# Bucket attention with a rational feed-forward layer on one core: row maxima transposed before they are clamped, bucket rows scaled on ScalarE, GpSimd's sums of exponentials made head by head

## Chip, cores and metric

The kernel runs on one core of one Trainium2 chip. The metric is the device time of one execution in microseconds (us). Three runs of the kernel before gave 1029.2, 1029.55 and 1035.9 us, median 1029.55 us.

## What is computed

Two stages follow each other. The first is attention within hash buckets, for 4 batches of 8 heads, 768 positions, 64 dimensions:

```python
q_bits = (np.einsum('bhsd,dk->bhsk', q, proj) > 0)        # 6 bits; k_bits the same
q_bucket = np.sum(q_bits * 2 ** np.arange(6), axis=-1)
mask = q_bucket[:, :, :, None] == k_bucket[:, :, None, :]
scores = np.where(mask, scale * (q @ k.T), -1e9)
scores = scores - np.max(scores, axis=-1, keepdims=True)
attn = np.exp(scores); attn = attn / (np.sum(attn, axis=-1, keepdims=True) + 1e-09)
x = attn @ v                                               # then heads side by side: 3072 x 512
```

The second is a feed-forward layer whose activation is a quotient of two polynomials:

```python
h = x @ w_in                                               # 512 -> 2048
g = (a0 + a1*h + a2*h*h + a3*h**3) / (1 + abs(b0)*abs(h) + abs(b1)*h*h + 1e-6)
out = g @ w_out                                            # 2048 -> 512
```

## The kernel before

**Pairs and steps.** The 32 heads are worked on as 16 pairs p = 0 to 15. A pair's attention takes 12 steps: step s is half `hf` of the queries (384 columns) and key tile `kt` (128 keys). In a step `scores` (L248) makes, for each of the two heads h, a product `pss` in PSUM, and ScalarE turns it into exponentials E (L256). GpSimd adds the exponentials of three key tiles into a tile `acc` (L263, one instruction for both heads, 128 x 768). `values` (L265) multiplies E by V into `psv`. In the middle pairs these come two steps at a time, so a group of eight `psv` records marks two steps on TensorE. `sums` (L284) adds up `acc` over the partitions into `psu`, once for each pair.

**The mask and the maximum ride in the product.** Operand tiles Q1 and K1 hold 64 rows of q or k, 12 rows of bucket bits scaled by plus or minus 2^60 (L209), and one row more, row 76, with the shift that is subtracted from the scores (L242). `bits` (L188) makes the bucket rows of two pairs at once, in every second pair: 16 small products into `psb`, then on VectorE a comparison out of PSUM into the tile `mb` (L202) and a multiplication of `mb` in place by a column of constants (L203). `maskrows` (L205) copies the rows into Q1 and K1 by DMA.

**The shift.** `maxstep` (L212) makes unmasked-scale products `psm` a pair and more ahead, and a VectorE reduction writes the row maxima into a tile M[p], 128 x 12 (L220; m in the profile). Its PSUM pool has two buffers, so TensorE's second next `psm` waits for a reduction. Then three functions follow:

- `shift_clamp` (L223): VectorE limits the maxima from below and negates them, SBUF to SBUF, into a tile nm of 128 x 12;
- `shift_turn` (L231): TensorE transposes nm into a PSUM tile `pst` of 12 x 128 (L234), ScalarE copies it to the tile mt (L236);
- `shift_rows` (L238): a DMA lays mt out as row 76 of Q1.

For pair 0 the three run twice, on one half of the queries each (`hf` 0 and 1, tiles of 128 x 6), since its maxima are made in another order (L433).

**Weights beside it.** `weights` (L319), spread over the steps, splits the weights into a high and a low part: two ScalarE passes, then on VectorE three integer passes (tiles wr and ws, L339 to L345), a ScalarE cast, and a subtraction (L351, to wi_lo or wr). There are two such sets for each pair. Also on VectorE are the low parts `lo` of q and k (L174), with two SBUF inputs.

**What sets the order.** Every compute instruction is kept in program order on its engine. The order comes from a table `plan`: `at(p, s, f)` files the call f under 12p + s, and the calls are made in order of that number, within one number in order of filing. For pair p the table has maxima 0 to 11 from step 7 of pair p-2 on (L373), the clamp at step 7 of pair p-1, the turn at step 8 and the DMA at step 10 (L400 to L402). For pair 0 the second half's clamp stands at 0.5 and its turn at 2 (L438 to L440).

**The second stage** (`Ffn`, L507) starts when attention is over; its 128 steps keep TensorE at work without the functions above.

In the profile nearly every instruction has line L61, that of the helper `issued` (L60 to L61); it is read by the names of the tiles, where numbers of buffers are left out. The functions that the diff touches:

Of the kernel before, what the change touches and what calls it, by code (L numbers as in the profile page):

```python
# [7 lines left out]
F32 = mybir.dt.float32  # L8
# [3 lines left out]
AF = mybir.ActivationFunctionType  # L12
ALU = mybir.AluOpType
# [4 lines left out]
P = 128  # L18
S = 768
HQ = 384  # L20
NT = S // P
# [13 lines left out]
CLAMP = 2.0 ** 40  # L35
# [30 lines left out]
def move(nc, out, in_, queue=None):  # L66

    (queue or nc.sync).dma_start(out.bitcast(F32), in_.bitcast(F32))
# [69 lines left out]
def attention(ctx, tc, nc, raw, ps_b, tail, tokens, early, operands_to_terms, ffn, load, QF, KF, v, w_in, w_out, wo_d, ident, cst, ones, prj,  # L138
# [9 lines left out]
    sm = ctx.enter_context(tc.tile_pool(name="sm", bufs=1))  # L148
# [5 lines left out]
    Q1, Q2, K1, K2, LO, V, M, MB, ACC, EXP, AV, MS = ({} for _ in range(12))  # L154

    def load_v(p, queue=nc.sync):
        V[p] = operand("v", p, [P, NT, P], F32)
        queue.dma_start(V[p], v[p])
# [8 lines left out]
    def high_move(p):  # L167
        for T, g in ((Q1[p], 0), (K1[p], 1)):
            move(nc, T[0:64, 1 - g, :], T[64:128, g, :])

    def low(p, t, engine=nc.vector):
        F, T = ((QF, Q1), (KF, K1))[t]
        LO[p, t] = raw.tile([P, S], F32R, tag=f"lo{t}", name=f"lo{t}_{p}", bufs=1)
        engine.tensor_tensor(out=LO[p, t], in0=F[p], in1=T[p][:, t, :].bitcast(F32), op=ALU.subtract)  # L174
# [13 lines left out]
    def bits(p, which=(0, 1)):  # L188

        if which[0] == 0:  # L190
            mb = sm.tile([P, 2, HQ], F32R, tag="mb", name=f"mb{p}")
            MB[p], MB[p + 1] = (mb, 0), (mb, 64)
        mb = MB[p + which[0]][0]
        sl = slice(64 * which[0], 64 * which[-1] + 64)
        ps = ps_a.tile([P, 2, 512], F32, tag="psa", name=f"psb{p}_{which[0]}")
        for hf in range(2):
            for w in which:
                for t, F in enumerate((QF[p + w], KF[p + w])):
                    o = 64 * w + 32 * t
                    nc.tensor.matmul(ps[o : o + 32, hf, 0:HQ], prj[:, t, :], F[:, hf * HQ : hf * HQ + HQ], start=True, stop=True)  # L200
        rows = mb[sl]
        nc.vector.tensor_scalar(out=rows, in0=ps[sl, :, 0:HQ], scalar1=0.0, scalar2=cst[sl, 0:1], op0=ALU.is_gt, op1=ALU.subtract)  # L202
        nc.vector.tensor_scalar(out=rows, in0=rows.bitcast(F32), scalar1=cst[sl, 1:2], scalar2=None, op0=ALU.mult)  # L203

    def maskrows(p, queues=(None, None)):  # L205
        mb, o = MB.pop(p)
# [13 lines left out]
        nc.vector.tensor_reduce(out=M[p][:, j : j + 1], in_=ps[:, :, 0:HQ], axis=AX.XY, op=ALU.max)  # L220


    def shift_clamp(p, hf=None):  # L223
        m = M[p].rearrange("p (h f i) -> p h f i", h=2, f=2)
        m = m if hf is None else m[:, :, hf : hf + 1, :]
        n = NT if hf is not None else 2 * NT
        MS[p] = sm.tile([P, n], F32, tag="nm", name=f"nm{p}_{hf}")
        nc.vector.tensor_scalar(out=MS[p].rearrange("p (h f i) -> p h f i", h=2, i=NT // 2), in0=m, scalar1=-CLAMP, scalar2=-1.0,
                                op0=ALU.max, op1=ALU.mult)

    def shift_turn(p, hf=None):  # L231
        n = NT if hf is not None else 2 * NT
        ps = ps_b.tile([P, 512], F32, tag="s", bufs=3, name=f"pst{p}_{hf}")
        nc.tensor.transpose(ps[0:n, 0:P], MS.pop(p), ident)  # L234
        MS[p] = sm.tile([n, P], F32R, tag="mt", name=f"mt{p}_{hf}")
        nc.scalar.copy(MS[p], ps[0:n, 0:P])  # L236

    def shift_rows(p, hf=None):  # L238
        cs = slice(0, S) if hf is None else slice(hf * HQ, hf * HQ + HQ)
# [8 lines left out]
    def scores(p, s):  # L248
        hf, kt = divmod(s, NT)
        e = EXP[p, s] = E[(12 * p + s) % len(E)]  # L250
        ks, qs = slice(kt * P, kt * P + P), slice(hf * HQ, hf * HQ + HQ)
        for h in range(2):
            ps = ps_b.tile([P, 512], F32, tag="s", bufs=3, name=f"pss{p}_{s}_{h}")
            nc.tensor.matmul(ps[:, 0:HQ], K1[p][0:77, h, ks], Q1[p][0:77, h, qs], start=True, stop=False)
            nc.tensor.matmul(ps[:, 0:HQ], K2[p][:, h, ks], Q2[p][:, h, qs], start=False, stop=True)
            nc.scalar.activation(e[:, h, 0:HQ], ps[:, 0:HQ], AF.Exp, scale=1.0 / 8.0)  # L256
        n = NT // PARTS
        if kt % n == 1:
            ACC[p, hf, kt // n] = sm.tile([P, 2, HQ], F32, tag="acc", name=f"acc{p}_{hf}_{kt // n}", bufs=ACCS)
        if kt % n > 0:  # L260
            acc = ACC[p, hf, kt // n]
            x = EXP[p, s - 1][:, :, 0:HQ] if kt % n == 1 else acc
            nc.gpsimd.tensor_tensor(out=acc, in0=x, in1=e[:, :, 0:HQ], op=ALU.add)  # L263

    def values(p, s):  # L265
        hf, kt = divmod(s, NT)
# [94 lines left out]
    def at(p, s, f, *args):  # L361
        plan.setdefault(12 * p + s, []).append((f, args))

    def spread(p, steps, gen):
        for s in steps:
            at(p, s, lambda g: next(g, None), gen)

    for p in range(NPAIR):
        for s in range(12):
            at(p, s, scores, p, s)  # L370

            if p > 1:
                at(p - 2, 7 + s if p > 2 else 9 + 0.85 * s, maxstep, p, s)  # L373

            if not 0 < p < NPAIR - 1:
                at(p, s + 2.3, values, p, s)
            elif s % 2:
                at(p, s + 1.3, values, p, s - 1)
                at(p, s + 1.3, values, p, s)
            if s % NT == NT - 1:  # L380
                at(p, s + (1.3 if 0 < p < NPAIR - 1 else 2.3), values_out, p, s // NT)
        for hf in range(2):
            at(p, 6 * hf + 9, values_store, p, hf)
        if p < NPAIR - 1:
            at(p, 14.5, sums, p)
            at(p, 16, sums_store, p)
        if p > 1:
            for t in range(2):
                at(p - 2, t, high, p, t)
                at(p - 2, 2 + t, low, p, t)  # L390
            if p % 2 == 0:
                at(p - 2, 3 if p == 2 else 2, bits, p)
            at(p - 2, 2, high_move, p)
            at(p - 2, 6 if p == 2 else 4, maskrows, p)
        if p > 0:
            at(p - 1, 0, second_low, p)
            at(p - 1, 3, second_high, p)
            at(p - 1, 4, load_v, p)
            d = 1.5 if p == 1 else 0
            at(p - 1, 7 + d, shift_clamp, p)  # L400
            at(p - 1, 8 + d, shift_turn, p)
            at(p - 1, 10 if d == 0 else 9.6, shift_rows, p)  # L402
        if p > 3:
            at(p - 4, 6, load, p)
        if p % NHP == NHP - 1 and p + 1 < NPAIR:
            spread(p, (20, 22, 23), recips(p // NHP))
# [12 lines left out]
    for t in range(2):  # L419
        high(0, t)  # L420
        low(0, t)
    bits(0, (0,))
    high_move(0)
    maskrows(0, (nc.sync, nc.scalar))
    load(2, nc.scalar)
    load_v(0, nc.scalar)
    bits(0, (1,))
    for t in range(2):
        high(1, t)
    second_low(0)  # L430
# [5 lines left out]
        at(-2, when[s], maxstep, 0, order[s])  # L436
        at(0, 0.6 + 0.7 * s, maxstep, 1, s)
    for hf in range(2):  # L438
        for s, f in ((5, shift_clamp), (6.5, shift_turn), (6.6, shift_rows)):
            at(-2, 19.5 * hf + s, f, 0, hf)  # L440
    for t in range(2):
        low(1, t, nc.gpsimd)
# [211 lines left out]
```

## Time and profile before

| | |
|---|---|
| median of three runs | 1029.55 us (1029.2 to 1035.9) |
| profiled execution | 1029.27 us, its span 1027.5 us |
| TensorE busy | 977.0 us (95%) |
| VectorE busy | 907.9 us (88%) |
| ScalarE busy | 678.9 us (66%) |
| GpSimd busy | 384.8 us (37%) |
| mean granted TensorE clock | 0.971 |

The names of the engines in the profile are PE (TensorE matmul), PEld (its weight loads), DVE (VectorE), ACT (ScalarE), POOL (GpSimd) and SP (the engine that issues most DMAs). The span has three parts: about 55 us of start, in which pair 0's operands are made and its first scores come; the attention proper to about 490 us; and the second stage to the end. A row of a timeline reads: start, duration, engine, operation, output <- inputs, shapes, count, and in brackets how long the engine had been idle and what released it. A row of the groups reads: shapes and count, then busy us and mean ns of one, then idle time before them. A row of windows gives for each engine its busy us and (x) its instructions, then the granted clock (PEclk, 1.00 is full), the DMA share and GB/s.

### The profile page before, as it was taken

What the parts mean: (1) busy time and instruction counts of PE and PEld (TensorE: products, weight loads), DVE (VectorE), ACT (ScalarE), POOL (GpSimd) and SP (SyncE); (2) the same over time, 40 slices, a digit from 0 to 9 for tenths busy, and PEclk for the clock granted to TensorE, in tenths of its full rate; (3) what the DMA queues carried; (4) which work ended last, traced back from release to release, by engine and by line L of the source; (5) the groups of instructions that cost most, each with busy time, mean ns of one, the idle gap of its engine ahead of it and who ended that gap; (6) DMA issues with size and microseconds to landing.
All of it is one profiled execution on the core that took longest, in us unless ns stands there. A gap on an engine that the chain in (4) does not pass through costs nothing.

```text
span 1027.5 us, 14486 instructions
## 1 busy us (share of the span) xinstructions
PE 977.0 (95%) x5009; PEld 749.4 (73%) x5009; DVE 907.9 (88%) x1207; ACT 678.9 (66%) x1419; POOL 384.8 (37%) x268
## 2 busy tenths in 40 slices
PE   6899988989898988999999999999999999999998
PEld 2565555555555555564999999999999999999996
DVE  5688788878978787767999999999999999999996
ACT  1466555656656655567877777777777777777775
POOL 1255554545545454556222222222222222222222
PEclk7799999999999999899999999999999999999999
DMA  7765564656656664673740201101111010020000
GB/s 202 195 165 175 165 177 124 177 163 186 187 165 211 206 205 134 177 217 118 283 137 15 69 11 62 32 1 62 32 57 36 1 62 31 1 72 22 32 1 31
DMA packets 50489, 112.95 MB, mean 110 GB/s; under 512 B 9296, under 2 KB 21968, under 8 KB 50416
## 3 DMA queue, kind: packets, MB, share of 16 engines
q1 hardware_dynamic: 49580, 110.59, 35.8%
q10 hardware_dynamic: 836, 1.44, 0.5%
q8 instruction: 39, 0.64, 0.3%
q14 instruction: 34, 0.28, 0.1%
HBM read 56.82 MB, written 21.17 MB: 76 GB/s over the span
## 4 chain that ended last, share of the span: by engine, by line
PE 78%; DVE 13%; DMA 3%; issue 2%; ACT 2%; SPq 1%; DVEq 0%; ACTq 0%
PE psh L61 26%; PE pso L61 26%; PE psv L61 10%; PE pss L61 9%; PE psm L61 4%; DVE m L61 3%; DVE wr L61 2%; DVE ws L61 2%; DVE nm_None L61 2%; PE psu L61 2%; DVE wi_lo L61 2%; ACT E L61 1%; DMA k<-k 1%; PE psb L61 1%; SPq L61 1%
## 5 line engine op out<-in xcount | busy, mean ns | idle before, releaser
L61 POOL TENSOR_TENSOR gl<-c,gh 128x384 fp32r<-128x384 f32 x128 | 140.6, 1099 | 396.0 <-ACT gh L61 369.4
L61 DVE TENSOR_REDUCE m<-psm 128x1 f32<-128x768 f32 x192 | 180.1, 949 | 76.8 <-PE psm L61 76.2
L61 PE MATMUL pso<-wo,gh 128*128 128x512 f32 x768 | 241.1, 395 | 0.0
L61 ACT ACTIVATE E<-pss 128x384 f32<-128x384 f32 x384 | 168.4, 490 | 97.9 <-PE pss L61 92.4
L61 POOL TENSOR_TENSOR acc<-E,E 128x768 f32<-128x768 f32 x64 | 126.2, 1972 | 190.3 <-ACT E L61 190.3
L61 PE MATMUL pss<-q,k 77*128 77x384 f32 (+1 forms) x768 | 183.1, 361 | 3.0 <-DMA q<-mt 2.6
L61 PEld LDWEIGHTS pss<-q,k 77*128 77x128 f32 (+1 forms) x768 | 136.7, 196 | 64.6 <-issue 54.4
L61 PE MATMUL psh<-xl,wi_hi 128*128 128x384 f32 x512 | 172.1, 336 | 0.0
L61 PE MATMUL psh<-xh,wi_hi 128*128 128x384 f32 x512 | 171.7, 335 | 0.0
L61 PE MATMUL psh<-xh,wi_lo 128*128 128x384 f32 x512 | 171.5, 335 | 0.0
L61 PEld LDWEIGHTS pso<-wo,gh 128*128 128x128 f32 x768 | 142.9, 188 | 23.7
L61 PE MATMUL psv<-E,v 128*64 128x385 f32 x768 | 157.3, 529 | 0.0
L61 PE MATMUL pso<-wo,gl 128*128 128x512 f32 x384 | 152.2, 396 | 0.3 <-POOL gl L61 0.3
L61 DVE SCALAR_TENSOR_TENSOR c<-c,ab,r 128x384 f32<-128x384 f32 x128 | 147.1, 1149 | 0.0
L61 ACT ACTIVATE h<-psh 128x384 f32<-128x384 f32 x128 | 63.1, 493 | 122.4 <-PE psh L61 122.4
L61 POOL TENSOR_TENSOR acc<-acc,E 128x768 f32<-128x768 f32 x64 | 113.9, 1780 | 30.1 <-ACT E L61 27.5
L61 PE MATMUL psm<-k,q 76*128 76x384 f32 x384 | 111.1, 374 | 13.9 <-DVE m L61 9.8
L61 PEld LDWEIGHTS psh<-xh,wi_hi 128*128 128x128 f32 x512 | 96.1, 188 | 6.3 <-issue 1.2
L61 PEld LDWEIGHTS psh<-xl,wi_hi 128*128 128x128 f32 x512 | 96.0, 188 | 5.1
L61 PEld LDWEIGHTS psh<-xh,wi_lo 128*128 128x128 f32 x512 | 96.1, 188 | 0.0
L61 PEld LDWEIGHTS psm<-k,q 76*128 76x128 f32 x384 | 71.7, 204 | 31.8 <-DVE m L61 22.2
L61 PEld LDWEIGHTS psv<-E,v 128*64 128x64 f32 x768 | 47.6, 141 | 64.1 <-issue 56.7
(63 smaller groups left out, 1322.6 us busy)
## 6 DMA issues: line engine op xcount, KB each, us to landing
q<-q SPq DMA_DIRECT2D x48, 192.0 KB
k<-k SPq DMA_DIRECT2D x48, 192.0 KB
wr<-w_in SPq DMA_DIRECT2D x16, 512.0 KB
wr<-w_out SPq DMA_DIRECT2D x16, 512.0 KB
wo_d<-wr SPq DMA_DIRECT2D x16, 512.0 KB
wo<-wo_d SPq DMA_DIRECT2D x16, 512.0 KB
q<-lo SPq DMA_DIRECT2D x32, 192.0 KB
k<-lo SPq DMA_DIRECT2D x32, 192.0 KB
```

The costliest lines, as they stand in the source:

```text
L61: return self.tc.keep_in_program_order(issue(*args, **kwargs))
```

## The change

1. **Turn, then clamp.** `shift_clamp` is gone. `shift_turn` transposes the maxima themselves, and a VectorE instruction clamps and negates them on the way out of PSUM, in place of ScalarE's copy. For pair 0's halves a VectorE copy first picks 6 of the 12 columns.
2. **Scaling on ScalarE.** The multiplication of the bucket rows becomes a ScalarE activation in a function `penalties`, one step after `bits`.
3. **Sums by heads.** GpSimd adds each head's 384 columns by an instruction of its own.

```diff
-        rows = mb[sl]
-        nc.vector.tensor_scalar(out=rows, in0=ps[sl, :, 0:HQ], scalar1=0.0, scalar2=cst[sl, 0:1], op0=ALU.is_gt, op1=ALU.subtract)
-        nc.vector.tensor_scalar(out=rows, in0=rows.bitcast(F32), scalar1=cst[sl, 1:2], scalar2=None, op0=ALU.mult)
+        nc.vector.tensor_scalar(out=mb[sl], in0=ps[sl, :, 0:HQ], scalar1=0.0, scalar2=cst[sl, 0:1], op0=ALU.is_gt, op1=ALU.subtract)
+
+    def penalties(p, which=(0, 1)):
+        sl = slice(64 * which[0], 64 * which[-1] + 64)
+        rows = MB[p + which[0]][0][sl]
+        nc.scalar.activation(rows, rows.bitcast(F32), AF.Identity, scale=cst[sl, 1:2])
...
-    def shift_clamp(p, hf=None):
-        m = M[p].rearrange("p (h f i) -> p h f i", h=2, f=2)
-        m = m if hf is None else m[:, :, hf : hf + 1, :]
-        n = NT if hf is not None else 2 * NT
-        MS[p] = sm.tile([P, n], F32, tag="nm", name=f"nm{p}_{hf}")
-        nc.vector.tensor_scalar(out=MS[p].rearrange("p (h f i) -> p h f i", h=2, i=NT // 2), in0=m, scalar1=-CLAMP, scalar2=-1.0,
-                                op0=ALU.max, op1=ALU.mult)
-
     def shift_turn(p, hf=None):
-        n = NT if hf is not None else 2 * NT
+        n, m = 2 * NT, M[p]
+        if hf is not None:
+            n, m = NT, sm.tile([P, NT], F32, tag="nm", name=f"nm{p}_{hf}")
+            nc.vector.tensor_copy(m.rearrange("p (h i) -> p h i", h=2), M[p].rearrange("p (h f i) -> p h f i", h=2, f=2)[:, :, hf, :])
         ps = ps_b.tile([P, 512], F32, tag="s", bufs=3, name=f"pst{p}_{hf}")
-        nc.tensor.transpose(ps[0:n, 0:P], MS.pop(p), ident)
+        nc.tensor.transpose(ps[0:n, 0:P], m, ident)
         MS[p] = sm.tile([n, P], F32R, tag="mt", name=f"mt{p}_{hf}")
-        nc.scalar.copy(MS[p], ps[0:n, 0:P])
+        nc.vector.tensor_scalar(out=MS[p], in0=ps[0:n, 0:P], scalar1=-CLAMP, scalar2=-1.0, op0=ALU.max, op1=ALU.mult)
...
-            x = EXP[p, s - 1][:, :, 0:HQ] if kt % n == 1 else acc
-            nc.gpsimd.tensor_tensor(out=acc, in0=x, in1=e[:, :, 0:HQ], op=ALU.add)
+            x = EXP[p, s - 1] if kt % n == 1 else acc
+            for h in range(2):
+                nc.gpsimd.tensor_tensor(out=acc[:, h, :], in0=x[:, h, 0:HQ], in1=e[:, h, 0:HQ], op=ALU.add)
...
                 at(p - 2, 3 if p == 2 else 2, bits, p)
+                at(p - 2, 4 if p == 2 else 3, penalties, p)
...
-            at(p - 1, 7 + d, shift_clamp, p)
             at(p - 1, 8 + d, shift_turn, p)
...
     bits(0, (0,))
+    penalties(0, (0,))
...
     bits(0, (1,))
+    penalties(0, (1,))
...
-        for s, f in ((5, shift_clamp), (6.5, shift_turn), (6.6, shift_rows)):
+        for s, f in ((6.5, shift_turn), (6.6, shift_rows)):
             at(-2, 19.5 * hf + s, f, 0, hf)
```

How this moves instructions is shown at three places.

**VectorE, steps 6 to 8 of pair 2**, where the maxima of pair 3 (m3) are complete and those of pair 4 begin. ISA is one of the passes over the weights. Before:

```order
L61 SCALAR_TENSOR_TENSOR ws4_870<-ws4_870,wr4_869 128x512
L61 TENSOR_REDUCE m3_743<-psm3_11_989 128x1
L61 ISA ws4_870<-wr4_869,ws4_870 128x1024
L61 TENSOR_SCALAR nm3_None_1016<-m3_743 128x12
L61 TENSOR_REDUCE m4_1018<-psm4_0_1019 128x1
L61 TENSOR_REDUCE m4_1018<-psm4_1_1040 128x1
```

And now:

```order
L61 SCALAR_TENSOR_TENSOR ws4_883<-ws4_883,wr4_882 128x512
L61 TENSOR_REDUCE m3_752<-psm3_11_1005 128x1
L61 ISA ws4_883<-wr4_882,ws4_883 128x1024
L61 TENSOR_REDUCE m4_1033<-psm4_0_1034 128x1
L61 TENSOR_SCALAR mt3_None_1054<-pst3_None_1052 12x128
L61 TENSOR_REDUCE m4_1033<-psm4_1_1056 128x1
```

The clamp has moved behind the first reduction of the next pair, and its input is now the transposed tile in PSUM, so that it follows TensorE where it used to go ahead of it.

**TensorE at the same place.** Before, and below it now:

```order
L61 MATMUL psm4_0_1019<-k1_4_867,q1_4_842 128x384 x2
L61 MATMUL pss2_8_0_1027<-q1_2_290,k1_2_313 128x384
L61 MATMUL pss2_8_0_1027<-q2_2_563,k2_2_564 128x384
L61 MATMUL pss2_8_1_1031<-q1_2_290,k1_2_313 128x384
L61 MATMUL pss2_8_1_1031<-q2_2_563,k2_2_564 128x384
L61 MATMUL pst3_None_1036<-cst_76,nm3_None_1016 12x128
```

```order
L61 MATMUL psm4_0_1034<-k1_4_880,q1_4_854 128x384 x2
L61 MATMUL pss2_8_0_1042<-q1_2_290,k1_2_312 128x384
L61 MATMUL pss2_8_0_1042<-q2_2_569,k2_2_570 128x384
L61 MATMUL pss2_8_1_1046<-q1_2_290,k1_2_312 128x384
L61 MATMUL pss2_8_1_1046<-q2_2_569,k2_2_570 128x384
L61 MATMUL pst3_None_1052<-cst_76,m3_752 12x128
```

The order is the same; the transposition's input is m3 itself, complete since the reduction of psm3_11, and no longer the clamped nm3.

**VectorE at the start, second half of pair 0** (m0, nm0_1), among the maxima of pair 1 (m1) and the low part of pair 2's q (lo0_2). Before:

```order
L61 TENSOR_REDUCE m0_215<-psm0_11_292 128x1
L61 TENSOR_SCALAR nm0_1_296<-m0_215 128x6
L61 TENSOR_REDUCE m1_298<-psm1_0_299 128x1
L61 TENSOR_REDUCE m1_298<-psm1_1_318 128x1
L61 TENSOR_TENSOR lo0_2_331<-qf2_182,q1_2_290 128x768
L61 TENSOR_REDUCE m1_298<-psm1_2_335 128x1
L61 TENSOR_REDUCE m1_298<-psm1_3_348 128x1
```

And now:

```order
L61 TENSOR_REDUCE m0_215<-psm0_11_292 128x1
L61 TENSOR_REDUCE m1_296<-psm1_0_297 128x1
L61 TENSOR_REDUCE m1_296<-psm1_1_317 128x1
L61 TENSOR_TENSOR lo0_2_331<-qf2_182,q1_2_290 128x768
L61 TENSOR_REDUCE m1_296<-psm1_2_335 128x1
L61 COPY nm0_1_339<-m0_215 128x6
L61 TENSOR_SCALAR mt0_1_343<-pst0_1_341 6x128
L61 TENSOR_REDUCE m1_296<-psm1_3_350 128x1
```

The instruction that feeds pair 0's second transposition has moved from ahead of lo0_2 to behind it and behind one more reduction; TensorE's order there is as it was (psm1_2, the transposition pst0_1, psv0_0, psm1_3).

## Prediction

> **What bounds the kernel now.** I read the windows first, to see which stage is filled by which engine.
>
> ```profile
> 55.00:445.00 390.00, 356.03 (x1952) 219.37 (x1952) 322.74 (x339) 230.57 (x512) 201.63 (x109) 0.96 0.60 175
> 445.00:490.00 45.00, 44.61 (x248) 25.17 (x237) 32.83 (x29) 31.38 (x71) 28.01 (x15) 1.00 0.52 164
> 490.00:1027.00 537.00, 533.50 (x2667) 480.43 (x2665) 517.10 (x798) 399.08 (x803) 140.63 (x128) 1.00 0.15 49
> ```
>
> The last 537 us are TensorE without a gap (533.5 busy, full clock) and hold nothing that is changed. From 55 to 445 us TensorE is idle for 34 us and its clock averages 0.96. That stage is where time can be won. The waits say what TensorE idles for:
>
> ```profile
> PE pst_None L61 <- DVE nm_None L61: 23.4, 13, 1.9
> PE psm L61 <- DVE m L61: 9.8, 18, 0.8
> DVE m L61 <- PE psm L61: 76.2, 47, 4.0
> ```
>
> 23.4 us, 13 times, up to 1.9 us each, are transpositions that wait for the clamp. The third row is the other direction: VectorE waits 76 us for products, so on the whole it follows TensorE. The timeline at one of the 13 places shows why the clamp is late:
>
> ```profile
> 307.81 0.87 ACT L61 ACTIVATE E<-pss 128x384 f32<-128x384 f32 x2
> 308.17 0.87 PE L61 MATMUL pss<-q,k 77*128 77x384 f32 x4
> 308.75 1.97 POOL L61 TENSOR_TENSOR acc<-E,E 128x768 f32<-128x768 f32 x1 [2.92 <-ACT E L61]
> 308.98 1.77 DVE L61 TENSOR_SCALAR nm_None<-m 128x12 f32<-128x12 f32 x1
> 310.67 1.85 DVE L61 TENSOR_REDUCE m<-psm 128x1 f32<-128x768 f32 x2
> 310.90 0.27 PE L61 MATMUL pst_None<-cst,nm_None 128*12 128x128 f32 x1 [1.87 <-DVE nm_None L61]
> 311.20 0.26 ACT L61 CAST mt_None<-pst_None 12x128 fp32r<-12x128 f32 x1 [0.73 <-PE pst_None L61]
> ```
>
> TensorE ends pss at 309.04 and could turn the maxima there. The clamp, over 12 columns, lasts 1.77 us and ends at 310.75, with GpSimd's addition (308.75 + 1.97 = 310.72). It is not work, it is held:
>
> ```profile
> L61 DVE TENSOR_SCALAR nm_None<-m x15: 160/1775/1779, 53.8 to 454.7; 128x12 f32<-128x12 f32 x15
> L61 DVE TENSOR_SCALAR mb<-psb,cst x9: 1004/1006/1023, 8.9 to 383.4; 128x768 fp32r<-128x768 f32 x7, 64x768 fp32r<-64x768 f32 x2
> L61 DVE TENSOR_SCALAR mb<-mb,cst x9: 612/994/996, 9.9 to 384.4; 128x768 fp32r<-128x768 f32 x7, 64x768 fp32r<-64x768 f32 x2
> ```
>
> (minimum, median, maximum in ns.) The same clamp takes 160 ns when free and 1775 when held. Of the two passes over mb, the one out of PSUM always takes 1.0 us, the one within SBUF 612 or 994. So a VectorE instruction of this kind that reads SBUF waits for a running GpSimd addition, and one that reads PSUM does not.
>
> The wait has a second price. These are windows of 3.41 us each:
>
> ```profile
> 162.97:166.38 3.41, 1.56 (x10) 0.98 (x10) 3.41 (x5) 2.06 (x6) 2.84 (x2) 1.00 0.47 173
> 166.38:169.80 3.42, 3.42 (x11) 1.60 (x8) 0.81 (x1) 0.01 (x1) 0.79 (x1) 0.50 0.03 9
> 193.69:197.10 3.41, 1.91 (x11) 0.82 (x11) 3.11 (x3) 1.33 (x4) 3.01 (x2) 1.00 0.58 205
> 197.10:200.51 3.41, 3.41 (x20) 2.56 (x20) 1.97 (x3) 2.49 (x6) 0.66 (x1) 1.00 0.01 2
> ```
>
> Where the clamp's wait falls so that TensorE is busy for 1.56 of 3.41 us, the next window has half the clock; where 1.91 us are left it has not. Over 55 to 445 us the mean of 0.96 means 2 x 0.04 x 390 = 31 us at half clock, nine such windows. What one costs is seen in the starts of the psv groups, two steps apart:
>
> ```profile
> 275.99 1.51 PE L61 MATMUL psv<-E,v 128*64 128x385 f32 x8
> 281.88 2.33 PE L61 MATMUL psv<-E,v 128*64 128x385 f32 x8
> 287.21 1.51 PE L61 MATMUL psv<-E,v 128*64 128x385 f32 x8
> 292.04 1.51 PE L61 MATMUL psv<-E,v 128*64 128x385 f32 x8
> 295.79 1.51 PE L61 MATMUL psv<-E,v 128*64 128x385 f32 x8
> ```
>
> The last distance, 3.75 us, is undisturbed. The first, 5.89, holds the transposition and its wait; the second, 5.33, the half clock; the third, 4.83, a wait for reductions that came late after it.
>
> **The change part by part.**
>
> *Turn, then clamp.* The transposition now waits for the maxima alone, which were complete one VectorE pass before 308.98. Its PSUM buffer is that of an exponential of the row at 307.81, free at 308.68, before pss ends. So the 23.4 us go: **-23.4**. The new clamp is nearest in size to ScalarE's copy of the same tile, 0.26 us, and reads PSUM, so it is not held. In VectorE's queue it stands behind a reduction of 0.95 us that starts at about 309.0, and the transposition (309.05 + 0.27) is done before that ends. No wait is added there, and the DMA that lays out the shift is ready at about 310.3 instead of 311.46.
>
> *The clock.* Without the 1.9 us holes no window falls to 1.6 us of work; the next largest waits are 0.8. Nine windows at half speed lose 31 x 0.5 = 15.6 us: **-15.6**. Below that it is nothing, if the holes are not what halves the clock; above, 2.6 a window (5.33 + 4.83 - 2 x 3.75), counted partly in the next term.
>
> The Trainium skill (TensorE: Matmul & The Clock Gate, "What's actually happening") has the clock halved after at least one idle window of about 3.4 us. By that rule waits of 1.9 us cost no clock and this term is nothing. The rows above disagree, since a window with 1.56 us of work was enough; the rule is kept as a rival below.
>
> *GpSimd's halves.* The group rows bound a piece of 384 columns:
>
> ```profile
> L61 POOL TENSOR_TENSOR gl<-c,gh 128x384 fp32r<-128x384 f32 x128 | 140.6, 1099 | 396.0 <-ACT gh L61 369.4 <-PE psh L61 19.1 <-issue 7.5
> L61 POOL TENSOR_TENSOR acc<-E,E 128x768 f32<-128x768 f32 x64 | 126.2, 1972 | 190.3 <-ACT E L61 190.3
> L61 POOL TENSOR_TENSOR acc<-acc,E 128x768 f32<-128x768 f32 x64 | 113.9, 1780 | 30.1 <-ACT E L61 27.5 <-ACT absb L61 1.1
> ```
>
> Between 0.89 (half of 1780) and 1.10; I take 1.0. 256 x 1.0 is 256 us for 240 now (126.2 + 113.9), over a stage in which GpSimd is half idle, and the first half starts one exponential (0.43 us) earlier: no cost; without that cover 16 us. The gain is on VectorE:
>
> ```profile
> 301.33 2.20 POOL L61 TENSOR_TENSOR acc<-E,E 128x768 f32<-128x768 f32 x1 [1.90 <-ACT E L61]
> 301.77 2.32 DVE L61 TENSOR_TENSOR wr<-ws,wr 128x512 fp32r<-128x512 f32 x1
> 305.01 0.61 PE L61 MATMUL psm<-k,q 76*128 76x384 f32 x2 [0.55 <-DVE m L61]
> L61 DVE TENSOR_TENSOR wr<-ws,wr x16: 680/689/2329, 287.1 to 487.3; 128x512 fp32r<-128x512 f32 x16
> ```
>
> A pass of 0.69 us (median) lasts 2.32 behind an addition, the reduction behind it is late, and psm waits 0.55 us for its buffer. Held by half an addition, the pass ends about 0.7 us earlier, more than that wait. The waits for m are 9.8 us in all, some of them the aftermath of half clocks. Bounds 0 (the halves run on without letting VectorE in between) and 9.8; I take two thirds: **-6.5**.
>
> The Trainium skill (SBUF — State Buffer, "Who interferes with whom") says that whoever issues first holds the shared port pair for the whole instruction. By it VectorE gets in between two halves, and the term would be the full 9.8.
>
> *Scaling on ScalarE.* VectorE loses nine passes of 0.6 to 1.0 us. ScalarE gains nine, nearest to its cast of a 128x768 tile:
>
> ```profile
> L61 ACT CAST q<-qf 128x768 fp32r<-128x768 f32 x16 | 13.3, 832 | 10.3 <-DMA k<-mb 8.1 <-DMA qf<-qT 2.2
> 328.03 1.86 ACT L61 ACTIVATE E<-pss 128x384 f32<-128x384 f32 x4
> 329.60 0.79 SPq L61 DMA_DIRECT2D q<-mb  x1
> ```
>
> The new pass stands behind the second of those exponentials (328.96), so mb is ready at 329.8 and SP, which issues its copies at 329.60 and has loads for pairs far ahead queued behind them, is 0.2 us late. The next exponentials wait 0.83 us; ScalarE is busy 231 of 390 us, which covers it. Taken at nothing; uncovered, 9 x 0.83 = 7.5 us.
>
> *The start.* Here the change costs. Pair 0's second half is clamped early today, and now its copy stands behind lo0_2:
>
> ```profile
> 34.40 0.41 PE L61 MATMUL pst<-cst,nm 128*6 128x128 f32 x1
> 34.74 1.55 PE L61 MATMUL psv<-E,v 128*64 128x385 f32 x4
> 36.51 0.96 DVE L61 TENSOR_TENSOR lo<-qf,q 128x768 fp32r<-128x768 f32 x1 [2.84 <-DMA q<-mt]
> 37.39 1.82 DVE L61 TENSOR_REDUCE m<-psm 128x1 f32<-128x768 f32 x2
> 12.78:40.09 27.31, 22.74 (x66) 14.59 (x70) 16.96 (x20) 7.45 (x14) 7.12 (x4) 0.50 0.89 218
> ```
>
> lo0_2 waits for a DMA until 36.51. Behind it come one reduction (to 38.3) and the copy of six columns, so the transposition goes at about 38.5 instead of 34.40, and psv, the next maxima, psb and VectorE's mb wait behind it in TensorE's queue: 4.1 us. TensorE is at half clock until 40.09; an idle stretch of 4 us puts the release off, by one window (1.7 us lost) to three (5.1). ScalarE's longer first scaling adds 0.2. VectorE's dropped pass gives 0.6 back. Bounds: +3, and +17.5 if all of a stretch as long as the quoted 27.3 us ran at half clock again (4 + 13.6). I take **+5.5**.
>
> **Sum**, against the profiled 1029.3 us (span 1027.5 and some 2 around it; the median, 1029.55, is the same): 1029.3 - 23.4 - 15.6 - 6.5 + 5.5 = 989.3, and 1 us for small waits at the new joints: **990 us**. VectorE's share does not rise: 323 us less 20 (clamp), 7 (mb) and some 10 of holding is 286, of 350 instead of 390.
>
> **The rivals.**
>
> *VectorE takes over.* With TensorE 10% faster, five reductions and four passes over weights follow each other in steps 8 to 12 with little room; TensorE then waits 1 us a pair for maxima, 13 us, and the 6.5 are not won: 1029.3 - 39 + 5.5 + 13 = 1009. For it: the wr pass of 2.32 us. Against it: the 76 us that VectorE waits.
>
> *The clock stays as it is* (the skill's rule): 990 + 15.6 = 1006. Against it: the windows.
>
> *The new clamp blocks VectorE: slower.* Every reduction behind it waits for the transposition, which waits behind pss for exponentials from ScalarE. If it comes x us after the reduction ahead of it, each of 13 pairs is x later, and clock and maxima are not won: 1029.3 + 5.5 - 23.4 + 13x. From x = 1.4 that is slower than before, from 2.2 by over 1%; at 2.5, 1044 us. Against it: the buffer free at 308.68, 0.4 us before it is needed.
>
> **How the numbers follow.** Forecast 0.70, VectorE takes over 0.17, the clock 0.08, slower 0.05. The forecast's own range is 980 to 1000, from its bounds; to leave out no more than 2 in 10 the range goes to 1009 above and, with all of 9.8 and 2.6 us a window, to 977 below. A measurement of this kernel tells about 1% from no change. Faster by more than that: 0.70 + 0.08 and most of 0.17, 0.92; within 1%: 0.04; slower: 0.04 (the slower rival with x under 2.2 lies within 1%).
>
> **What would show it.** Right: no wait of pst for VectorE after 60 us; psv groups 3.75 us apart except where psu, psb or pst lie between; granted clock 1.00 from 50 us to the end; mt on VectorE near 0.26 us each; acc pieces near 1.0; one hole of 4 us on TensorE ahead of pst near 38 us. Wrong: waits of psm for m over 10 us, half-clock windows that remain, a VectorE queue that stands before mt, or a start that is longer by over 10 us.

## The result, and the profile after

The change takes 982.62 us (median of four runs, 981.05 to 984.5) against 1029.38 us of the kernel before in the same series (four runs, 1029.13 to 1035.9). The ratio is 0.9532, with a 95% interval of 0.9491 to 0.9573: faster by 4.7%, forecast 990 us. The profiled execution has a span of 980.3 us (before 1027.5) and a mean granted clock of 0.983 (before 0.971).

The windows of the changed kernel answer to those of before: the attention proper and the second stage.

```profile
55.00:402.00 347.00, 344.07 (x1991) 219.08 (x1991) 263.92 (x338) 234.47 (x516) 251.34 (x220) 1.00 0.69 200
443.00:980.00 537.00, 533.34 (x2666) 480.39 (x2664) 516.81 (x798) 398.69 (x803) 140.40 (x128) 1.00 0.15 49
```

The second stage is as long as it was. From 55 us on TensorE is idle for 3 us where it was idle for 34, and its clock is full. VectorE's share of that stretch fell from 323 of 390 us to 264 of 347. Its waits:

```profile
PE pst L61 <- DVE nm L61: 4.5, 2, 3.2
PE psm L61 <- DVE m L61: 3.3, 8, 0.7
DVE m L61 <- PE psm L61: 90.4, 72, 3.2
```

The 13 waits of `pst_None` are gone; the two that are left are pair 0's, at the start. Waits for maxima fell from 9.8 to 3.3 us, and VectorE waits longer for TensorE than before (90 us, where it was 76). The timeline at one of the places where the clamp used to stand:

```profile
256.65 1.98 POOL L61 TENSOR_TENSOR acc<-E,E 128x384 f32<-128x384 f32 x2 [0.92 <-ACT E L61]
257.13 0.27 PE L61 MATMUL pst_None<-cst,m 128*12 128x128 f32 x1
257.51 0.27 DVE L61 TENSOR_SCALAR mt_None<-pst_None 12x128 fp32r<-12x128 f32 x1
```

The transposition goes without a wait, in the middle of the first half of an addition, and the clamp out of PSUM follows at once. The groups of the tiles that the change touches (shortest, median and longest in ns):

```profile
L61 DVE TENSOR_SCALAR mt_None<-pst_None x15: 266/268/279, 59.2 to 408.5; 12x128 fp32r<-12x128 f32 x15
L61 POOL TENSOR_TENSOR acc<-E,E x128: 992/1028/1771, 31.9 to 435.0; 128x384 f32<-128x384 f32 x128
L61 POOL TENSOR_TENSOR acc<-acc,E x128: 857/1016/1727, 33.9 to 437.6; 128x384 f32<-128x384 f32 x128
```

The new clamp is never held (266 to 279 ns). A half is 1.0 us at the median, but some last 1.7: there VectorE holds GpSimd, as rows further down show. The starts of the psv groups, two steps apart:

```profile
275.09 1.51 PE L61 MATMUL psv<-E,v 128*64 128x385 f32 x8
278.86 1.51 PE L61 MATMUL psv<-E,v 128*64 128x385 f32 x8
282.85 1.52 PE L61 MATMUL psv<-E,v 128*64 128x385 f32 x8
286.63 1.51 PE L61 MATMUL psv<-E,v 128*64 128x385 f32 x8
```

3.77, 3.99 with the transposition in it, 3.78: where 5.89, 5.33 and 4.83 stood. The start, in the timeline:

```profile
35.67 0.96 DVE L61 TENSOR_TENSOR lo<-qf,q 128x768 fp32r<-128x768 f32 x1 [2.10 <-DMA q<-lo]
37.41 0.16 DVE L61 COPY nm<-m 128x6 f32<-128x6 f32 x1
37.72 0.37 PE L61 MATMUL pst<-cst,nm 128*6 128x128 f32 x1 [3.23 <-DVE nm L61]
38.02 1.55 PE L61 MATMUL psv<-E,v 128*64 128x385 f32 x4
```

The row of lo is lo0_2. `pst` comes behind it, at 37.72 instead of 34.40, and the half clock lasts from 12.6 to 43.3 us instead of 12.8 to 40.1. The 25th psv product, clear of this, starts at 56.01 (before 52.68), so the start costs 3.3 us; from there to the first psh the change takes 381.1 us and the kernel before 431.6. The gain of the steady part is 50.5 us.

### The profile page after: what moved, and what is told of

It reads as the page before. It is cut to its first block, busy times and chain, and to the rows that moved or that the text cites. A ratio compares the mean times of both kernels' runs of the same rounds, so it can differ in the third digit from the quotient of the medians.

```text
span 980.3 us, 14803 instructions
## 1 busy us (share of the span) xinstructions
PE 957.6 (98%) x5009; PEld 744.8 (76%) x5009; DVE 835.4 (85%) x1200; ACT 679.2 (69%) x1411; POOL 436.8 (45%) x396
## 4 chain that ended last, share of the span: by engine, by line
PE 92%; DVE 3%; DMA 3%; ACT 1%; SPq 0%; issue 0%; ACTq 0%; DVEq 0%
PE psh L61 27%; PE pso L61 27%; PE pss L61 15%; PE psv L61 13%; PE psm L61 6%; PE psu L61 2%; DVE m L61 1%; PE psb L61 1%; DMA wr<-w_out 1%; DMA q<-lo 0%; SPq L61 0%; DVE c L61 0%; DMA v<-v 0%; DMA prj<-proj 0%; DMA q<-mt 0%
## 5 line engine op out<-in xcount | busy, mean ns | idle before, releaser
L61 POOL TENSOR_TENSOR acc<-E,E 128x384 f32<-128x384 f32 x128 | 150.9, 1199 | 113.9 <-ACT E L61 113.9
L61 PE MATMUL pss<-q,k 77*128 77x384 f32 (+1 forms) x768 | 180.2, 357 | 2.5 <-DMA q<-mt 1.5
L61 PEld LDWEIGHTS pss<-q,k 77*128 77x128 f32 (+1 forms) x768 | 134.0, 192 | 60.3 <-issue 50.1
L61 PE MATMUL psv<-E,v 128*64 128x385 f32 x768 | 148.3, 503 | 0.0
L61 POOL TENSOR_TENSOR acc<-acc,E 128x384 f32<-128x384 f32 x128 | 142.7, 1135 | 7.8 <-ACT E L61 5.9
L61 PE MATMUL psm<-k,q 76*128 76x384 f32 x384 | 107.8, 365 | 7.0 <-DMA k<-mb 3.7
L61 ACT ACTIVATE c<-psh,ab 128x384 f32<-128x384 f32 x128 | 86.5, 676 | 1.7 <-POOL gl L61 1.7
```

The source lines that it names most:

```text
L61: return self.tc.keep_in_program_order(issue(*args, **kwargs))
```

## The experiments

All ratios are against runs of the kernel before on the same chip.

| kernel | edit | median us | ratio, 95% interval |
|---|---|---|---|
| the change | turn, scaling, halves | 982.62 | 0.9532 (0.9491 to 0.9573) |
| turn alone | before, turned then clamped | 995.31 | 0.9658 (0.9629 to 0.9688) |
| halves alone | before, sums by heads | 977.86 | 0.9506 (0.9454 to 0.9558) |
| scaling alone | before, scaling on ScalarE | 1006.86 | 0.9774 (0.9738 to 0.9811) |
| turn and scaling | the change without halves | 989.96 | 0.9603 (0.9573 to 0.9633) |
| sooner | before, clamp one reduction earlier | 991.05 | 0.9626 (0.9598 to 0.9653) |
| halves, later | halves, clamp one reduction later | 985.73 | 0.9588 (0.9551 to 0.9624) |
| early start | change, pair 0 turned ahead of lo0_2 | 981.89 | 0.9549 (0.9515 to 0.9582) |
| two holes' reductions | change, pst waits for two more | 1041.88 | 1.0103 (1.0037 to 1.0169) |
| halves, sooner | halves, clamp one reduction earlier | 979.53 | 0.9513 (0.9495 to 0.9530) |
| halves and scaling | the change without the turn | 979.54 | 0.9510 (0.9487 to 0.9533) |
| no additions | before, acc set once | 975.20 | 0.9472 (0.9451 to 0.9492) |
| one reduction | change, pst waits for one more | 1004.83 | 0.9765 (0.9741 to 0.9788) |

### The parts, each alone

My theory was the prediction's: the turn brings most of the gain, the halves some, the scaling none. The rivals gave the gain to another part. *Turn alone* has the diff's `shift_clamp` and `shift_turn` and nothing else; *turn and scaling* leaves out only the sums by heads.

```diff
-        nc.tensor.transpose(ps[0:n, 0:P], MS.pop(p), ident)
+        nc.tensor.transpose(ps[0:n, 0:P], m, ident)
...
-        nc.scalar.copy(MS[p], ps[0:n, 0:P])
+        nc.vector.tensor_scalar(out=MS[p], in0=ps[0:n, 0:P], scalar1=-CLAMP, scalar2=-1.0, op0=ALU.max, op1=ALU.mult)
```

> Only the turn ahead of the clamp; bucket rows scaled on VectorE and whole additions on GpSimd, as before. Theory (the clamp is held by an addition, the transposition waits for it, and the holes that this makes on TensorE halve the clock): the 23.4 us of waits and the half-clock windows (16 us) go, the start is 3.4 us longer, and the waits of psm for maxima, about 10 us, stay: 993 us, clock 1.00 from 50 us on. Rival 1 (the clock was halved by something else): 1009 us, windows at 0.50 remain. Rival 2 (the gain comes from shorter additions): within 10 us of before.

> The whole change but for GpSimd's additions, which stay whole. Theory: against the change the waits of psm for maxima come back, 8 to 10 us: 991 us. Rival (once the clamp reads PSUM, the length of an addition decides nothing): 983 us, as the change.

995.31 and 989.96 us: within 2.3 us of the forecast for both. The waits of `pst_None` are gone in both, and the clock is full from 46.6 and 46.5 us; waits of psm for m stay (10.6 us in 20, 8.7 us in 16). From the 25th psv product to the first psh *turn alone* takes 392.4 us, 39.2 less than the kernel before. The 5.4 us between the two kernels were not expected: on top of the turn, scaling on ScalarE does bring something.

*Halves alone* is this edit:

```diff
-            x = EXP[p, s - 1][:, :, 0:HQ] if kt % n == 1 else acc
-            nc.gpsimd.tensor_tensor(out=acc, in0=x, in1=e[:, :, 0:HQ], op=ALU.add)
+            x = EXP[p, s - 1] if kt % n == 1 else acc
+            for h in range(2):
+                nc.gpsimd.tensor_tensor(out=acc[:, h, :], in0=x[:, h, 0:HQ], in1=e[:, h, 0:HQ], op=ALU.add)
```

> Only GpSimd's additions head by head; clamp ahead of the transposition as before. Theory: the clamp is held for half an addition, its median falls from 1.78 to about 0.9 us, the holes of 1.9 us become about 1 us, too short for the clock, and the waits of psm for maxima go: 12 + 16 + 8 us less, 993 us with no cost at the start. Rival (what counts is that the clamp stands on the path, not how long it is held): only the waits for maxima go, 1020 us.

977.86 us, the largest gain of the three, where I had expected a clamp held by half an addition. The clamp, still where it was, is free in all but one of the pairs: median 158 ns, once 980. Its timeline:

```profile
303.52 0.16 DVE L61 TENSOR_SCALAR nm_None<-m 128x12 f32<-128x12 f32 x1
303.75 1.98 POOL L61 TENSOR_TENSOR acc<-E,E 128x384 f32<-128x384 f32 x2 [0.90 <-ACT E L61]
```

It starts 0.23 us before the addition (x2: its two halves in one row). In the kernel before it started 0.23 us after it (308.98 and 308.75). The exception is pair 2, where the clamp starts 0.07 us behind the addition:

```profile
76.65 1.98 POOL L61 TENSOR_TENSOR acc<-E,E 128x384 f32<-128x384 f32 x2 [0.96 <-ACT E L61]
76.72 0.98 DVE L61 TENSOR_SCALAR nm_None<-m 128x12 f32<-128x12 f32 x1
```

It is held for one half, to 77.70, and not for the two, which last to 78.63.

*Scaling alone* was a surprise as well:

```diff
-        nc.vector.tensor_scalar(out=rows, in0=rows.bitcast(F32), scalar1=cst[sl, 1:2], scalar2=None, op0=ALU.mult)
+        nc.scalar.activation(rows, rows.bitcast(F32), AF.Identity, scale=cst[sl, 1:2])
```

> Only the scaling of the bucket rows on ScalarE. Theory: nine VectorE passes less, none of them ahead of a product that waits, and the holes stay: 1026 to 1030 us. Rival (VectorE's work as such bounds the attention, so what it loses is won): 7.8 us less, 1021 us.

1006.86 us, 23 us less, where theory and forecast said nothing. `pst_None` waits 7 times instead of 13, 12.3 us in all. The two kinds of pair, one that has a scaling pass and one that has none, in its timeline:

```profile
274.24 0.16 DVE L61 TENSOR_SCALAR nm_None<-m 128x12 f32<-128x12 f32 x1
274.27 1.83 POOL L61 TENSOR_TENSOR acc<-E,E 128x768 f32<-128x768 f32 x1 [1.97 <-ACT E L61]
...
300.44 1.96 POOL L61 TENSOR_TENSOR acc<-E,E 128x768 f32<-128x768 f32 x1 [2.92 <-ACT E L61]
300.66 1.78 DVE L61 TENSOR_SCALAR nm_None<-m 128x12 f32<-128x12 f32 x1
```

0.03 us ahead of the addition the clamp takes 0.16 us; 0.22 us behind it, 1.78.

### A race lost by 0.2 us

So the prediction's account of the wait was not the whole of it. The new theory: clamp and addition race for something that only one of them can have, the clamp loses in the kernel before by 0.2 us, and whatever brings VectorE forward by that much frees it, whether it touches the clamp or not. The Trainium skill (SBUF — State Buffer, "Who interferes with whom") says of VectorE's two-port modes that whoever issues first gets the shared port pair for the whole instruction and the other fully blocks. The rows just quoted agree, with 0.16 us on the one side and 1.78 on the other; that the clamp runs in such a mode no row shows. The rival: the halves gain because the additions are shorter. *Sooner* changes nothing but the clamp's place in the order, for pairs 3 to 15:

```diff
-            at(p - 1, 7 + d, shift_clamp, p)
+            at(p - 1, 6 if p > 2 else 7 + d, shift_clamp, p)
```

> The kernel before, with the clamp of pairs 3 to 15 one VectorE pass (0.67 us) earlier in VectorE's queue, and nothing else. New theory (a lost race: the clamp starts 0.2 us after an addition that holds the port; whatever brings it ahead of that start frees it): clamp at 0.16 us, the waits of pst and the half-clock windows go but for pairs 1 and 2, the waits of psm for maxima stay: 992 us. Rival (with GpSimd adding half of the time the clamp meets an addition wherever it stands, so only shorter additions or a PSUM source help): 1015 us or more, median of the clamp above 0.8 us.

991.05 us, one line for 38 us. Its timeline at one pair:

```profile
286.12 0.17 DVE L61 TENSOR_SCALAR nm_None<-m 128x12 f32<-128x12 f32 x1
286.39 2.17 POOL L61 TENSOR_TENSOR acc<-E,E 128x768 f32<-128x768 f32 x1 [2.92 <-ACT E L61]
```

The race is won by 0.27 us, `pst_None` waits once in 15 (1.2 us), and no half clock is left after the start. The theory stands for whole additions. *Halves, later* turns it round: with the halves, the clamp moved behind one more reduction (7 to 7.5), so that it comes after the addition has begun.

```diff
-            at(p - 1, 7 + d, shift_clamp, p)
+            at(p - 1, 7.5 + d, shift_clamp, p)
```

> Additions head by head as in e2_halves, but the clamp one reduction (0.95 us) later, behind the addition's start. Race theory: the clamp loses again, is held for up to half an addition (median 0.5 to 1.0 us) and comes 1.0 to 1.8 us after pss ends: 13 us or more above e2_halves, 991 to 1000 us, clock 1.00 where the hole is under 1.8 us. Rival (halves end the holding by themselves): clamp at 0.16 us, the transposition only 0.5 us late, 984 us.

985.73 us, and the median clamp is 167 ns: it comes after the addition has begun and is still not held. The expectation of a held clamp fell, the rival's numbers hold:

```profile
309.68 1.98 POOL L61 TENSOR_TENSOR acc<-E,E 128x384 f32<-128x384 f32 x2 [0.89 <-ACT E L61]
310.56 0.17 DVE L61 TENSOR_SCALAR nm_None<-m 128x12 f32<-128x12 f32 x1
310.87 0.27 PE L61 MATMUL pst_None<-cst,nm_None 128*12 128x128 f32 x1 [0.53 <-DVE nm_None L61]
```

The clamp comes 0.88 us behind the start of the first half, just as that half ends, and runs at the joint of the two. So these rows don't show how long one that comes earlier would be held; pair 2 above does, with one half. What is left is that `pst_None` waits 0.5 us for a clamp behind a reduction (7.6 us in 13), which is the 8 us to *halves alone*. So the halves free the clamp twice over: VectorE comes earlier, and where it comes late it waits for one half at most.

### What the halves bring beyond the clamp

*Halves, sooner* puts the halves on top of *sooner*, where the clamp is free already:

> The halves with the old clamp, which for pairs 3 to 15 is called one reduction sooner. Theory (with the halves no clamp is held any more, so there is nothing left for an earlier clamp to win): the same as the halves alone, 976 to 980 us, ratio 0.950; clamp median 0.16 us; waits of psm for m about 2.7 us. Rival (the halves still leave VectorE short at some joints, and an earlier clamp frees the reductions behind it): 973 to 975 us, waits of psm for m under 1.5 us.

979.53 us, the same as the halves alone, as the theory has it. Against *sooner* it is 11.5 us less, and that is the halves' worth without the clamp, as long as the scaling stays on VectorE. In the timeline of *sooner*, the joint of two pairs:

```profile
201.03 1.52 PE L61 MATMUL psv<-E,v 128*64 128x385 f32 x8
201.38 2.21 POOL L61 TENSOR_TENSOR acc<-E,E 128x768 f32<-128x768 f32 x1 [3.75 <-ACT E L61]
201.81 2.33 DVE L61 TENSOR_TENSOR wi_lo<-ws,wi_hi 128x512 fp32r<-128x512 f32 x1
204.06 0.94 DVE L61 TENSOR_REDUCE m<-psm 128x1 f32<-128x768 f32 x1
205.06 0.62 PE L61 MATMUL psm<-k,q 76*128 76x384 f32 x2 [0.54 <-DVE m L61]
205.61 1.51 PE L61 MATMUL psv<-E,v 128*64 128x385 f32 x8
```

And the same joint in *halves, sooner*:

```profile
196.77 3.19 POOL L61 TENSOR_TENSOR acc<-E,E 128x384 f32<-128x384 f32 x2 [3.04 <-ACT E L61]
196.80 1.51 PE L61 MATMUL psv<-E,v 128*64 128x385 f32 x8
197.59 1.50 DVE L61 TENSOR_TENSOR wi_lo<-ws,wi_hi 128x512 fp32r<-128x512 f32 x1
199.01 0.95 DVE L61 TENSOR_REDUCE m<-psm 128x1 f32<-128x768 f32 x1
199.06 0.51 PE L61 MATMUL psm<-k,q 76*128 76x384 f32 x2
200.58 1.51 PE L61 MATMUL psv<-E,v 128*64 128x385 f32 x8
```

The subtraction is held for 0.8 us less, the reduction behind it is in time, psm doesn't wait, and the distance of the groups falls from 4.58 to 3.78. The wait reads 0.54 us, but it costs 0.80; the weight load of that product waits as well (0.87 us, at 205.06). There are twelve such joints. The six groups with psb in them fall from 5.5 to 5.25. 12 x 0.8 + 6 x 0.25 = 11.1.

The halves are not the only way to free these joints. *Turn alone* has twelve of 4.6 us, *turn and scaling* six of 4.4 to 4.6, and the change none. In *turn and scaling*, whose additions are whole, two joints that follow each other read:

```profile
103.97 0.69 DVE L61 TENSOR_TENSOR wi_lo<-ws,wi_hi 128x512 fp32r<-128x512 f32 x1
104.11 2.24 POOL L61 TENSOR_TENSOR acc<-E,E 128x768 f32<-128x768 f32 x1 [4.20 <-ACT E L61]
...
127.75 2.10 POOL L61 TENSOR_TENSOR acc<-E,E 128x768 f32<-128x768 f32 x1 [2.03 <-ACT E L61]
128.08 2.32 DVE L61 TENSOR_TENSOR wi_lo<-ws,wi_hi 128x512 fp32r<-128x512 f32 x1
```

It is the clamp's race over again: 0.14 us ahead of the addition the subtraction takes 0.69 us, 0.33 us behind it 2.32, and the joints that are free and those that are not take turns, as the pairs with and without a scaling pass do. Scaling on ScalarE wins it at every second joint, the halves at all of them.

*No additions* replaces each row of additions by one memset, so that the sums of exponentials are left out, and bounds what freeing VectorE can give.

```diff
-            nc.gpsimd.tensor_tensor(out=acc, in0=x, in1=e[:, :, 0:HQ], op=ALU.add)
+            if kt % n == 1:
+                nc.gpsimd.memset(acc, 1.0)
```

> The kernel before without GpSimd's additions: one memset of acc in place of each row of three, so the sums of exponentials are left out. It holds VectorE almost nowhere in the attention stage, so it bounds from below what freeing VectorE can give. Theory (the halves already give nearly all of it): 974 to 979 us, no wait of pst for nm, psm for m under 3 us, full clock from 43 us on. Rival (the holding costs more than the clamp's lost race, since passes over weights and reductions are also late): 960 to 970 us.

975.20 us; the clamp lasts 165 to 174 ns, psm waits for m 0.4 us. The halves leave some 3 us to win, no more; the rival (960 to 970) falls.

### What the rest of the change costs on top of the halves

*Halves and scaling* has the diff's second and third part and keeps `shift_clamp` and ScalarE's copy as before.

> The halves with the scaling on ScalarE, the maxima clamped and turned in the old order: the whole change without its turn. Theory (the turn is what costs the whole change its start of 3.4 us, and scaling adds a millisecond's thousandth or so to the joints): 978 to 981 us, half clock ending at 40 us as before, not at 43. Rival (what the whole change has more than the halves alone is owed to the scaling on ScalarE): 982 to 983 us, with waits for the longer ScalarE queue at the 7 pairs that have a scaling pass.

979.54 us. Its first psv stands at 34.29 us, where *halves alone* has 34.43 and the change 38.02: the turn alone makes the start late, as the theory says. After the start, the 25th to the 457th psv product take 226.8 us in the change, 227.3 in *halves alone* and 227.4 in *halves and scaling*. With the halves in place, turn and scaling bring nothing more there. The times of these kernels (977.9 to 982.6) lie so close that their intervals overlap; it is the starts in the traces that tell them apart.

*Early start* tries to win the start back:

```diff
-            at(-2, 19.5 * hf + s, f, 0, hf)
+            at(-2, (s, s + 18.9)[hf], f, 0, hf)
```

> The change, with the turn of pair 0's second half ahead of lo0_2 and of psm1_2. Theory (the change costs 3.4 us at the start, because that turn stands behind a VectorE instruction that waits for a DMA): pst at 34.5 instead of 37.7, clock full one window earlier, 979 us. Rival (the start is bounded by the DMA for lo0_2 in any case): 982.5 us, as the change.

981.89 us, no difference that the runs can tell. `pst` does come at 34.10, but other products are now ahead of psv, which starts at 36.32; the 25th psv product is at 54.83 (change 56.01), 1.2 us of the 3.3. The expectation missed.

### Is it the hole that halves the clock?

The change takes away holes and half clock together, and so cannot show by itself that the one brings the other. So I put holes back, without GpSimd having a part in them: the transposition of pairs 1 to 15 also takes columns that hold maxima of V, made on VectorE just before. This adds two:

```diff
-        nc.tensor.transpose(ps[0:n, 0:P], m, ident)
+        extra = 2 if hf is None else 0
+        for i in range(extra):
+            nc.vector.tensor_reduce(out=m[:, n + i : n + i + 1], in_=V[p], axis=AX.XY, op=ALU.max)
+        nc.tensor.transpose(ps[0 : n + extra, 0:P], m, ident)
```

> The change, with two VectorE reductions over V (0.86 us each, no port shared with GpSimd) ahead of each transposition of pairs 1 to 15, whose results ride along in two more columns and are not used. They make holes of 1.7 to 1.9 us on TensorE that GpSimd has no part in. Theory (holes of this size halve the clock in the next 3.4 us): 15 x 1.8 = 27 us of waits and windows at 0.50 after some of them, 8 to 16 us: 1018 to 1026 us. Rival (the clock needs a whole idle window): 1010 us and clock 1.00 throughout.

1041.88 us. The direction is right, the price higher than I forecast: +59 us at the median. The four runs lie apart, from 1035.97 to 1049.28 us, 53 to 67 us above the change; the profiled one is the longest, with 30.4 us of waits (15 times, up to 2.2 us). The windows at one of them, two of 3.4 us and the hole (2.15 us, ahead of 149.36) across their border:

```profile
145.40:148.80 3.40, 1.81 (x10) 1.49 (x9) 3.23 (x5) 2.69 (x7) 2.48 (x4) 0.99 0.85 265
148.80:152.20 3.40, 2.84 (x9) 1.30 (x11) 1.65 (x3) 0.00 (x0) 1.47 (x2) 0.50 0.54 197
```

Half clock follows a window in which TensorE was busy for more than half the time. The Trainium skill (TensorE: Matmul & The Clock Gate, "What's actually happening") puts the fall to half clock after at least one idle window of about 3.4 us; neither window here is one, and this run lost its clock at eleven places after the start. The rival that went by it (1010 us, full clock) falls. *One reduction* makes the hole smaller:

```diff
-        extra = 2 if hf is None else 0
+        extra = 1 if hf is None else 0
```

> The whole change with one more reduction of V on VectorE that each of pairs 1 to 15's transpositions waits for: a hole of 1 us on TensorE at each pair, half that of the kernel with two. Theory (a window needs a hole near 1.9 us to fall to 1.6 of 3.41 us busy): the clock stays full after the start, and the time is the change's plus 15 holes of 1.0 to 1.1 us, 996 to 1001 us. Rival (any new hole of 1 us beside the others is enough for the clock): half-clock windows at several pairs and 1010 to 1025 us.

1004.83 us, between the two: the theory's upper end is missed by 4 us, the rival's lower end by 5. The holes are 1.28 us at the mean (18.0 us in 14), not 1.0 to 1.1; 18 of the 22 us is the holes alone. The six runs go from 1002.94 to 1010.65 us. The three shortest, 20 to 21 us above the change, have a mean clock of 0.982 to 0.985, the change 0.983. The profiled run is the longest and has half clock at two places after the start. One of these in windows, and in the timeline:

```profile
136.10:139.51 3.41, 2.01 (x10) 1.41 (x9) 2.33 (x4) 2.78 (x7) 2.50 (x4) 0.99 0.91 292
139.53:142.94 3.41, 2.84 (x9) 1.30 (x11) 1.66 (x3) 0.00 (x0) 1.46 (x2) 0.50 0.43 159
```

```profile
137.51 0.59 PE L61 MATMUL psm<-k,q 76*128 76x384 f32 x2 [0.68 <-DMA k<-mb]
140.10 0.37 PE L61 MATMUL pst_None<-cst,m 128*13 128x128 f32 x1 [1.30 <-DVE m L61]
```

There a second hole of 0.68 us, a wait for a DMA, fell into the same window as the first part of the new one. At the other 13 pairs with a hole of 1.3 us the clock stayed full but at one, so such a hole alone seldom costs the clock; what set that one apart is open.

## Why the prediction was right, point by point

**Turn and clock (-23.4 and -15.6).** Right in size. *Turn alone* takes 39.2 us off the steady part (392.4 for 431.6), and *sooner*, which frees the clamp and does nothing else, takes 38.1 off the whole (1029.17 to 991.05), for the 39 of the two terms. The clock's term rests on holes, and holes put back bring half clock back. The sum of the two terms is shown, how it divides into waits and clock is not: no run takes away one and leaves the other. The working was right on what holds the clamp, but not that a fifth of a microsecond decides it: such an instruction "waits for a running GpSimd addition", as the prediction put it, but it need not meet a running one. That is why the terms do not belong to one edit each.

**GpSimd's halves (-6.5) and scaling on ScalarE (nothing).** Here the sum was off. Together the two bring 12.7 us on top of *turn alone* (995.31 to 982.62), where 6.5 was forecast. How the 12.7 divides depends on the order, since both free the same joints. With scaling first, scaling brings 5.4 and the halves 7.3 (995.31, 989.96, 982.62). With the halves first, scaling moves nothing that the runs can tell (977.86 and 979.54), and halves without scaling are worth 11.5. The halves' mechanism, a pass over weights held by half an addition and a reduction in time, is in the rows above, and VectorE does get in between two halves, so the lower of its bounds fell. The size was bounded by the waits of psm for m (9.8 us), but a wait of 0.54 us there costs 0.80 between groups, and the groups with psb gain as well. At the scaling the prediction looked at what hides ScalarE's new pass, and not at what a VectorE that comes earlier would meet: at six joints of *turn and scaling* the subtraction wins its race, and alone, where the clamp stands a fifth of a microsecond behind an addition, the edit takes 23 us off. The halves alone take 52 us off, since they also win the clamp its race; so in this change turn and halves are each enough for the 39 us.

**The start (+5.5).** Right in its mechanism: a transposition behind lo0_2, a hole of 3.23 us, half clock that lasts one window longer. Too high by 2.2 us for this kernel. lo0_2 began at 35.67 and not at 36.51, so the hole is 0.8 us shorter. And the window of half clock cost nothing of its own: the hole lies inside the stretch, and TensorE is busy in it for 22.6 us of 30.7 where it was busy for 22.7 of 27.3, so no more work ran at half clock than before. In *turn alone* and *turn and scaling* the 25th psv product stands at 57.95 and 58.23, 5.3 and 5.5 us late, as forecast, with half clock to 46.6 and 46.5; the halves, then, go with 2 us less at the start, and why is not shown.

**Joints (+1).** One wait that was not there shows: between the 457th and the 481st psv product the change takes 14.2 us, *halves alone* 12.8, where a pass over weights waits for a DMA of w_out. 1.4 us.

The sum was 7.4 us too high (990.3 before rounding). Followed from *turn alone* to the change, 0.5 us of that lies in turn, clock and start (forecast 1029.3 - 39 + 5.5 = 995.8, measured 995.31), 5.4 in the scaling, and 1.8 in halves and joints together (forecast 6.5 - 1 = 5.5, measured 7.3).

**The rivals.** VectorE did not take over: its waits for TensorE grew from 76 to 90 us. The clock did not stay as it was: 1.00 from 43.3 us on. The new clamp waited once, 1.5 us, for the transposition, and did not block VectorE. Of what was to show the prediction right, nearly all came. The hole ahead of pst is 3.2 us and not 4. The psv groups are 3.75 us apart, 3.9 to 4.2 with pst, 5.2 with psu or psb, except the one with the wait for w_out and three of 4.7, in pairs where small reciprocals stand ahead of a reduction on VectorE.

## What to carry to other kernels

Where an instruction has two durations and the long one ends together with another engine's, look at which of the two started first and by how much: here 0.2 us decided over 38 us, and moving one call by one place in the order was worth nearly as much as the rewrite. Run the parts of a change alone before crediting them: three edits that took 35, 52 and 23 us off alone took 47 off together, no more than the sums by heads alone. A hole on TensorE cost little more than itself at 1.3 us (22 us for 18.0), and 1.6 to 2.2 times itself at 1.9 to 2.2 us, since half clock often follows it (38 us for 23.4; 67 for 30.4 in the profiled run of *two holes' reductions*).

## What the runs showed of the hardware that was not expected

- A VectorE instruction that is held by GpSimd gets in between two GpSimd instructions that follow each other without a gap. The clamp of 76.72 us in *halves alone* ends at 77.70, within a row of two halves that lasts from 76.65 to 78.63; the subtraction of 197.59 in *halves, sooner* ends at 199.09, within one from 196.77 to 199.96.
- The holding goes both ways. In that last row the two halves take 3.19 us instead of 1.98: a subtraction with two SBUF inputs (lo, 196.73) began 0.04 us before the first of them, and that of 197.59 ran ahead of the second. GpSimd's busy time rose from 384.8 to 436.8 us with the same sums to make. About 17 us of that is an estimate of the pieces' own cost, from undisturbed rows of the start: 1.97 and 1.81 us for two halves (31.90 and 33.88 in the change), 1.83 and 1.68 for a whole addition (32.64 and 34.63 before), 64 of each kind.
- There is no sharp bound in TensorE's busy time for the half clock: 2.0 to 2.1 of 3.41 us busy was followed by it (*one reduction*), 1.91 in the kernel before was not. In all fourteen traces, from 55 to 485 us, with windows laid on the recorded changes of the clock, each of the 16 windows at full clock with up to 1.59 us busy was followed by half clock, and none with 2.2 us or more. In between both occur: 1.64 us from 418.42 in *two holes' reductions* was not followed by it, 2.08 us from 136.03 in *one reduction* was. It can then last long: from 139.5 to 149.7 us in *one reduction*, with TensorE busy for 9.6 us of that.
- The record of the granted clock can be wrong. In *halves, sooner* the windows show full clock at the start, and the products there are as slow as in *halves alone*, whose windows show half. The window of the first:

```profile
13.00:40.50 27.50, 23.59 (x70) 14.56 (x70) 17.68 (x21) 7.33 (x14) 7.42 (x6) 1.00 0.90 222
```

and of the second:

```profile
13.00:40.50 27.50, 23.68 (x70) 14.58 (x70) 17.06 (x20) 7.45 (x14) 7.42 (x6) 0.50 0.89 226
```

The products psm up to 45 us (shortest, median and longest in ns), again of the first:

```profile
L61 PE MATMUL psm<-k,q x38: 338/522/690, 13.1 to 44.1; 76*128 76x384 f32 x38
```

and of the second:

```profile
L61 PE MATMUL psm<-k,q x38: 336/522/690, 13.4 to 44.1; 76*128 76x384 f32 x38
```

So a mean clock of 1.00 in one run and 0.986 in another is no difference between them, unless the products' own durations show it.
